# From the sixth unit on, attention products in 64x32 tiles with a query per partition, and x turned by VectorE blocks and DMAs through DRAM

## The chip, the core and the metric

The kernel runs on one core of a Trainium2 chip. The metric is the device time of one execution in microseconds; lower is better. Three executions of the kernel before took 380.43, 379.7 and 379.51 us, so its median is 379.7 us.

## What is computed

Two layers run one after the other. The first is attention in chunks: 4 batches, 8 heads, 768 positions, head size 64. A chunk of 32 queries sees 64 keys: 16 positions to its left, its own 32, 8 to its right, and 8 memory keys. The second mixes channels: it takes the attention output as x with 512 channels, blends each position with the one before it, and multiplies by three weight matrices.

```python
# attention, per chunk of 32 queries
scores = scale * q_c @ k_full.T            # 32 x 64 per head
a = softmax(scores)
out[:, :, c] = a @ v_full                  # 32 x 64 per head
# channel mix, x is (batch, 768, 512)
xk = mu_k * x + (1 - mu_k) * x_prev
xr = mu_r * x + (1 - mu_r) * x_prev
k = maximum(xk @ w_k, 0)
v = k * k @ w_v
r = sigmoid(xr @ w_r)
return r * v
```

Everything is in float32. Attention products run as float32 matmuls. The channel mix runs from unit 1 on as three float32r matmuls each (high part by high, high by low, low by high), and from unit 2 on the product with `w_v` is cut into seven smaller products.

## The kernel before, in words

The 3072 positions are cut into 12 units of 256 (`UTOK`), each of two tiles of 128 positions; a batch has three units. For each unit the following is done.

- **Scores.** `scores(u)` multiplies queries by keys: 64 matmuls in 64x32 tiles of the array (`s`, L463). One matmul has 64 contraction rows, 32 queries as the weights that are loaded, and 64 keys as the columns that are streamed. The result takes two PSUM banks (tag `s`, one buffer). VectorE then takes the maximum (L476), subtracts it (L481), ScalarE takes the exponential (L487), VectorE sums (L491 to L493) and normalizes (L497). The result is `e`.
- **Turning e.** From unit 3 (`MOVED`) on, `move(u)` turns e so that keys lie on partitions: VectorE turns 32x32 blocks (`eT`, L706), one DMA writes them to DRAM (`eD`, L713), and four DMAs read them back into `aTz` (L717). `aTz` holds the attention weights in two halves, one for each half of the partitions, with zeros in the other half.
- **Attention products.** In `attention(t)`, `f_a` multiplies values by attention weights: 16 matmuls per tile in 128x64 tiles of the array (`px`, L640), two tiles per unit. The values are the loaded weights, so the result has a channel per partition and a query per column: it is x already turned as the channel mix needs it. ScalarE copies it from PSUM into `xT` (L286, `f_x`), with one more column for the position before the unit (L654).
- **Blending.** `prep(u)` takes the difference of neighbours (`df`, L771) and blends (`xf`, L782, four instructions for each of two blends), then makes the high and low parts `xh` and `xl` (L286/L288, L803).
- **Channel mix.** `channel_mix(u)` holds four blocks `h0` to `h3` (`ph`, L1250, the product with `w_k`), two blocks `g0` and `g1` (`pr`, L1139, the gate), and `products(u)` the seven products `p1` to `p7` with `w_v` (`accx`, `accy`, `accz`, L1041), followed by additions (L1080, L1083) and multiplications by the gate (L1106, L1111, L1113) on VectorE and the stores.

TensorE's order is written out by hand. `LEAD` gives it up to unit 1; after that `STAGES` gives one line per unit u, a stage: `s` are the scores of unit u + 2, `a` and `b` the attention products of the two tiles of unit u + 1, `h0` to `h3` and `p1` to `p7` belong to unit u, and `g0` and `g1` to unit u + 1. A planner (`Plan`) orders the other engines around this: it gives each operation an estimated duration and a due time, and places them one by one. Its order is fixed when the program is built; on the chip each engine runs its own queue in order and waits on semaphores. All DMAs are issued from SyncE's queue.

Of the kernel before, what the change touches and what calls it, by code (L numbers as in the profile page):

```python
# [16 lines left out]
P = 128  # L17
# [19 lines left out]
LEAD = "s0.0.0 s0.0.1 s0.1 t0 t1 a0 s1.0 a1 h0.0.0 h0.0.1 h0.1.0 h0.2.0 h0.3.0 s1.1 h0.3.1 g0.0.0 g0.1.0 g0.0.1 h0.3.2 h0.3.3 g0.1.1 t2 t3 v0.0.0 a2 a3 v0.1.0 s2.0 v0.1.1 v0.0.1 h1.0.0 h1.0.1 h1.0.2 h1.0.3 h1.1.0 h1.1.1 t4 t5 h1.1.2 h1.1.3 a4 a5 v1.0.0 s3.0 g1.0 g1.1 v1.0.1 g2.0 g2.1 v1.1.0 v1.1.1"  # L37
STAGES = {
# [7 lines left out]
MOVED = 3  # L46
ROWS = [(0, 0, 1), (0, 1, 1), (1, 0, 2), (2, 0, 2), (3, 0, 2)]
# [158 lines left out]

def te_order():
# [3 lines left out]
    for u in range(1, nu):  # L211
# [5 lines left out]
        own.update(a=("a", 2 * u + 2), b=("a", 2 * u + 3), t=("t", 2 * u + 2), w=("t", 2 * u + 3), s=("s", u + 2, 0))  # L217
# [17 lines left out]
def local_attention__then__channel_mix(  # L235
# [372 lines left out]
    def attention(t, o_n, e):  # L608
# [56 lines left out]
        da = due["a", t]  # L665
# [20 lines left out]
    moved = {}  # L686

# [10 lines left out]
    def move(u, o_n, e):  # L698
# [16 lines left out]
        def f_in(x):  # L715
            s, z = x // 2, slice(CHUNK * x, CHUNK * (x + 1))
            nc.sync.dma_start(  # L717
                aTz[z, s].rearrange("p i n -> p (i n)").rearrange("p (j n) -> p j n", j=NJ),
# [5 lines left out]
        o_free = prior["a"]  # L724
# [4 lines left out]
    mix = {}  # L729

# [33 lines left out]
    def prep(u):  # L764
        deps = [xdone[u * QPU + c] for c in range(QPU)]
        ds = Slot("x4")

        def f_df(e):
            x = T["xT", u]
            d = T["df", u] = sb("x4", [P, KT, UTOK], f"df{u}")  # L770
            e.tensor_sub(d, x[:, :, 1:], x[:, :, :UTOK])  # L771

        if u not in OWN:
            o_d = op(either(u > 2, dve=(1.15, True), pool=(2.0, True)), f_df, deps, new=[ds], use=[xslot[u]])
        for m in (1, 0) if u > 1 else (0, 1):
            last = m == (u <= 1)

            def f_mix(m=m, last=last):
                d = T["df", u]
                f = T["xf", u, m] = d if last else sb("x4", [P, KT, UTOK], f"xf{u}")  # L780
                for k in range(KT):
                    nc.vector.scalar_tensor_tensor(  # L782
# [36 lines left out]
            else:  # L819
                o_d = op(("dve", 1.59, True), f_mix, [o_d, o_mu], new=[] if last else [fs], use=[ds, xslot[u]])  # L820
# [640 lines left out]
```

## Time and profile before

| | |
|---|---|
| median of three runs | 379.7 us |
| the profiled execution, its own time | 379.66 us |
| its span | 377.7 us |
| granted TensorE clock | 0.999 |
| busy: TensorE / VectorE / ScalarE / GpSimd | 98% / 82% / 59% / 1% of the span |
| TensorE matmul busy | 371.2 us |

The span runs from the first to the last instruction that the profiler shows; the execution's own time is about 2.0 us more. Shares of busy time are means over the whole span. From stage 5 on, at 180.88 us, the kernel repeats a stage of 29.1 us per unit until the scores run out in stage 10.

### The profile page before, as it was taken

How to read it: one execution, taken by the hardware profiler on the slowest of the kernel's cores; microseconds unless marked ns; L12 is line 12 of the kernel's file. 1: busy time of each engine (PE TensorE's matmuls, PEld its weight loads, DVE VectorE, ACT ScalarE, POOL GpSimd, SP SyncE). 2: the span in 40 equal slices, each digit the busy share in tenths (PEclk: the TensorE clock that was granted, in tenths of full speed). 3: DMA queues.
4: the chain of work that ended last, by engine and by line, in shares of the span. 5: the costliest groups of instructions: out<-in, count | busy, mean ns of one | idle time of the engine just before them, and what ended most of it. 6: DMA issues, size and time to landing. Idle time of an engine off the chain costs nothing.

```text
span 377.7 us, 10682 instructions
## 1 busy us (share of the span) xinstructions
PE 371.2 (98%) x4702; PEld 343.9 (91%) x4702; DVE 310.2 (82%) x499; ACT 221.7 (59%) x330; POOL 3.2 (1%) x11
## 2 busy tenths in 40 slices
PE   8999999999998999999999999999999999999996
PEld 6785579889998999999999999999999999999996
DVE  4899999999899599499599689689779879588264
ACT  2788998772682574475376276276276277256350
POOL 2000000000000000000000000000000000000000
PEclk9999999999999999999999999999999999999999
DMA  8999972513533723632731731751651332200101
GB/s 312 417 407 409 367 256 102 165 61 129 182 111 108 256 88 112 225 113 76 260 114 62 265 123 59 220 170 57 210 182 58 113 115 98 70 3 0 57 2 56
DMA packets 19822, 58.43 MB, mean 155 GB/s; under 512 B 2240, under 2 KB 7232, under 8 KB 19392
## 3 DMA queue, kind: packets, MB, share of 16 engines
q1 hardware_dynamic: 19776, 57.75, 42.7%
q8 instruction: 37, 0.61, 0.7%
q14 instruction: 9, 0.07, 0.1%
HBM read 46.73 MB, written 11.01 MB: 153 GB/s over the span
## 4 chain that ended last, share of the span: by engine, by line
PE 90%; DVE 4%; DMA 3%; SPq 1%; ACT 1%; issue 0%; DVEq 0%
PE ph L1250 29%; PE pr L1139 14%; PE accy L1041 10%; PE accx L1041 6%; PE accz L1041 6%; PE px L640 6%; PE pv L1352 4%; PE s L463 4%; PE ph L1196 4%; DMA vw<-in_vw_dram 3%; PE ph L1225 3%; PE pv L1339 2%; PE pr L1130 2%; DVE al L986 1%; PE pt L620 0%
## 5 line engine op out<-in xcount | busy, mean ns | idle before, releaser
L1250 PE MATMUL ph<-xh,wk 128*128 128x256 f32 x320 | 89.8, 281 | 0.0
L1250 PE MATMUL ph<-xl,wk 128*128 128x256 f32 x320 | 88.0, 275 | 0.0
L1250 PE MATMUL ph<-xh,wl 128*128 128x256 f32 x320 | 88.0, 275 | 0.0
L1269 ACT ACTIVATE kf<-ph 128x512 f32<-128x512 f32 x41 | 24.5, 597 | 90.0 <-PE ph L1250 88.3
L1250 PEld LDWEIGHTS ph<-xh,wk 128*128 128x128 f32 x320 | 61.3, 192 | 1.4
L1250 PEld LDWEIGHTS ph<-xh,wl 128*128 128x128 f32 x320 | 61.4, 192 | 0.0
L1250 PEld LDWEIGHTS ph<-xl,wk 128*128 128x128 f32 x320 | 61.4, 192 | 0.0
L286 ACT CAST ah<-kf 128x512 fp32r<-128x512 f32 x43 | 25.9, 620 | 23.3 <-DVE kf L964 22.0
L986 DVE TENSOR_TENSOR al<-kf,ah 128x512 fp32r<-128x512 f32 x50 | 33.8, 682 | 0.0
L1139 PE MATMUL pr<-wr,xh 128*128 128x512 f32 x88 | 33.5, 381 | 0.0
L1139 PE MATMUL pr<-wr,xl 128*128 128x512 f32 x88 | 33.4, 380 | 0.0
L1139 PE MATMUL pr<-wl,xh 128*128 128x512 f32 x88 | 33.4, 379 | 0.0
L1276 ACT ACTIVATE kf<-kf 128x512 f32<-128x512 f32 x48 | 30.0, 628 | 1.1
L640 PEld LDWEIGHTS px<-aTz,vw 128*64 128x64 f32 x768 | 23.5, 138 | 2.7 <-ACT w L348 0.8
L640 PE MATMUL px<-aTz,vw 128*64 128x64 f32 x768 | 25.2, 224 | 0.4 <-DMA vw<-in_vw_dram 0.4
L1041 PE MATMUL accx<-wv,ah 128*128 128x256 f32 x80 | 22.0, 275 | 0.0
L1041 PE MATMUL accx<-wl,ah 128*128 128x256 f32 x80 | 22.0, 275 | 0.0
L1041 PE MATMUL accx<-wv,al 128*128 128x256 f32 x80 | 22.0, 275 | 0.0
L1271 DVE TENSOR_SCALAR kf<-ph 128x512 f32<-128x512 f32 x7 | 4.8, 692 | 20.4 <-PE ph L1250 20.4
L1148 ACT ACTIVATE sg<-pr 128x512 f32<-128x512 f32 x24 | 14.2, 596 | 10.5 <-PE pr L1139 10.3
L1139 PEld LDWEIGHTS pr<-wr,xl 128*128 128x128 f32 x88 | 16.6, 189 | 2.5 <-DVE xl L803 0.2
L1139 PEld LDWEIGHTS pr<-wr,xh 128*128 128x128 f32 x88 | 16.7, 190 | 1.9
(149 smaller groups left out, 965.5 us busy)
## 6 DMA issues: line engine op xcount, KB each, us to landing
qk<-in_qk_dram SPq DMA_DIRECT2D x23, 768.0 KB, 6.7
vw<-in_vw_dram SPq DMA_DIRECT2D x24, 512.0 KB, 4.6
out_dram<-o SPq DMA_DIRECT2D x23, 256.0 KB, 2.4
eD<-eT SPq DMA_DIRECT2D x9, 512.0 KB, 2.6
aTz<-eD SPq DMA_DIRECT2D x36, 128.0 KB, 2.9
raw<-in_w_v_dram SPq DMA_DIRECT2D x4, 1024.0 KB, 9.4
raw<-in_w_k_dram SPq DMA_DIRECT2D x3, 1024.0 KB, 13.2
raw<-in_w_r_dram SPq DMA_DIRECT2D x2, 1024.0 KB, 8.7
```

The lines of the kernel that those rows point to most:

```text
L286: e.copy(dst, src)
L463: nc.tensor.matmul(s5[CHUNK * j : CHUNK * (j + 1), h, d - c, r, :], *operands(ts[d], r, j, slice(64 * h, 64 * h + 64)), start=True, stop=True,
L640: nc.tensor.matmul(p3[64 * h : 64 * h + 64, 2 * g : 2 * g + 2, CHUNK * j : CHUNK * j + CHUNK], v[:, g, h, j, :], a[:, h, g, j, :], start=True,
L986: nc.vector.tensor_sub(low(n), place[n](), T["ah", u, n].bitcast(F32))
L1041: nc.tensor.matmul(o, x, w, start=(n in fresh and c + i == 0), stop=(c == cs[-1] and i == 2), skip_group_check=True)
L1139: nc.tensor.matmul(pairs(p), x[:, k, c * P : (c + 1) * P], woven(w), start=(k + n == 0), stop=(k == KT - 1 and n == 2),)
L1148: nc.scalar.activation(sg, p, AF.Sigmoid)
L1196: nc.tensor.matmul(p[:, i * UTOK + c * P : i * UTOK + (c + n) * P], T["w", id(wk_hl[0]), k][:, fc], T["xf", u, 0][:, k, z], start=(i + k + ...
L1250: nc.tensor.matmul(pairs(p[:, i * UTOK : (i + 1) * UTOK]), w[:, fc], x[:, :, k].rearrange("p t n -> p n t"), start=(k + n == 0), stop=(k = ...
L1269: e.activation(part(), p, AF.Relu)
L1276: e.activation(q, q, AF.Square)
L1352: nc.tensor.matmul(pairs(p), x[:, tc_], woven(w), start=(f + n == 0), stop=(f == FT - 1 and n == 2),)
```

## The change

Units 0 to 4 stay as they are. From unit 5 (`ROWX`) on:

- The attention products swap their operands. The attention weights are now the loaded weights (64 keys by 32 queries) and the values are streamed (64 columns), in 64x32 tiles, 64 matmuls per unit. The result `px` has a query per partition, and takes the two PSUM banks of tag `s`, which the scores use too (one buffer for both).
- x then has to be turned. `rows_to_columns(u)` does it as `move` does for e: VectorE turns 32x32 blocks from PSUM into the free half of `aTz`, one DMA writes them to DRAM (`xD`), four DMAs read them back into `xT`. ScalarE's copies of `px` go.
- Chunks are placed in another order in the inputs (`chunk_order`), so that a unit's x comes out in order. `xT` then has the layout (chunk group, channel block, 64 positions) without the extra column, so `df` is made by three instructions (within 64 positions, between groups, and the first position, which reads the unit before).
- In `STAGES`, `z` are the scores of unit u + 3 and `x` the products of unit u + 2: both come one stage earlier than before. Stage 2 has `s` and `z`, stage 3 has `a`, `b` and `x`.
- `e` arrives in the first half of `aTz` alone and has one buffer (`aT5`).
- `LEAD` and the order of the products within a stage are new: p2 moves ahead of p6.

```diff
-    0: "s h0 h1 a b h2 h3 p1 p7 g0 p6 g1 p5 p2 p4 p3",
-    2: "h0 h1 s h2 a b h3 p1 p7 g0 p6 g1 p5 p2 p4 p3",
-    10: "h0 a b h1 h2 h3 p1 p7 g0 p6 p4 p5 p2 p3",
-    11: "h0 h1 h2 h3 p1 p7 g1 p6 p4a p5 p4b p3 p2",
+    0: "z h0 h1 x h2 h3 p1 p7 g0 p2 p6 g1 p5 p4 p3",
+    2: "h0 h1 s h2 a b p1 h3 p7 g0 p6 g1 p2 z p4 p5 p3",
+    3: "h0 a b h1 h3 z h2 p1 p7 g0 x g1 p6 p5 p2 p4 p3",
+    4: "z h0 h1 x h2 h3 p1 p7 g0 p2 p6 g1 p5 p4 p3",
+    9: "h0 h1 x h2 h3 p1 z g0 p7 p6 g1 p5 p2 p4 p3",
+    10: "h1 h0 h2 h3 p1 g0 p7 p6 p4 p5 p2 p3",
+    11: "h1 h0 h2 h3 p1 p7 g1 p6 p4a p5 p4b p3 p2",
...
+ROWX = 5
...
+            if u >= ROWX:
+                vload[t] = lv, vs
+                if c:
+                    rows_to_columns(u, landed, az, due["a", 2 * u])
+                return
...
+    def rows_to_columns(u, landed, az, da):
...
+            p = T["px", u] = ps("s", f"px{u}", QPU)
+            p = p.rearrange("p (r g c h d) -> p r g c h d", r=2, g=2, c=QPU, h=2)
...
+            for c in range(QPU):
+                v = T["vw", ts[c]].rearrange("p (g h j d) -> p g h j d", g=2, h=2, j=NJ)
+                for g in range(2):
+                    for h in range(2):
+                        for j in range(NJ):
+                            for i in range(2):
+                                z = slice(64 * i, 64 * i + 64)
+                                nc.tensor.matmul(
+                                    p[CHUNK * j : CHUNK * (j + 1), i, g, c, h, :], a[z, c, h, g, j, :], v[z, g, h, j, :],
+                                    start=True, stop=True,
+                                )
...
+        def f_turn():
+            t = turned_x
+            nc.vector.transpose(
+                t.rearrange("p (x m q) -> p x m q", x=X, m=M), T["px", u].rearrange("p (m x k) -> p x m k", m=M, x=X)
+            )
...
+        def f_out():
+            T["xD", u] = dram.tile([P, M * X * CHUNK], F32, tag="xD", name=f"xD{u}")
+            nc.sync.dma_start(T["xD", u], turned_x)
...
+            nc.sync.dma_start(
+                rows(u)[CHUNK * x : CHUNK * (x + 1)].rearrange("p j k n -> p j (k n)"),
+                T["xD", u].rearrange("(j p) (x n) -> x p j n", j=NJ, x=X)[x],
+            )
...
+                e.tensor_sub(d[:, :, :, 1:], back[:, :, :, : n - 1], back[:, :, :, 1:])
+                e.tensor_sub(d[:, :, 1:, 0], back[:, :, : NJ - 1, n - 1], back[:, :, 1:, 0])
...
+                    e.tensor_sub(d[:, :, 0, 0], rows(u - 1)[:, NJ - 1, :, n - 1], back[:, :, 0, 0])
```

**TensorE in the middle of stage 6** (between h1 and h2; the names are PSUM and SBUF tiles with their buffer numbers, and the last figure is how many equal instructions follow each other). Before, the two tiles of unit 7:

```order
L1250 MATMUL ph_1_2936<-xl_0_2816,wk_71 128x256
L1250 MATMUL ph_1_2936<-xh_0_2797,wl_740 128x256
L640 MATMUL px_2965<-aTz,vw_2582 64x2x32 x16
L640 MATMUL px_2984<-aTz,vw_2619 64x2x32 x16
L1250 MATMUL ph_2_3010<-xh_0_2797,wk_68 128x256
```

Now, unit 8:

```order
L1360 MATMUL ph_1_3170<-xl_0_3060,wk_71 128x256
L1360 MATMUL ph_1_3170<-xh_0_3028,wl_740 128x256
L726 MATMUL px_3202<-vw_2848,aTz 32x64 x32
L726 MATMUL px_3202<-vw_2852,aTz 32x64 x32
L1360 MATMUL ph_2_3271<-xh_0_3028,wk_68 128x256
```

At the same place 32 matmuls into two PSUM tiles became 64 matmuls into one.

**VectorE at the end of stage 5 and the start of stage 6.** Before, from the last addition after p5 (`o_1<-accy`) to the maximum of the next scores:

```order
L1083 TENSOR_TENSOR o_1_2722<-accy_2727,o_1_2722 128x256
L1111 TENSOR_TENSOR o_0_2695<-accx_2665,sg_2322 128x256
L803 TENSOR_TENSOR xl_0_2816<-df_2623,xh_0_2797 128x1024
L1083 TENSOR_TENSOR o_1_2722<-accz_2682,o_1_2722 128x256
L1106 TENSOR_TENSOR o_1_2722<-o_1_2722,sg_2322 128x512
L1083 TENSOR_TENSOR o_0_2695<-accy_2727,o_0_2695 128x256
L1113 TENSOR_TENSOR o_0_2695<-o_0_2695,sg_2322 128x256
L474 MEMSET s_0_2833 32x2x4x8
L476 TENSOR_REDUCE mx_0_2928<-s_0_2833 128x16
```

Now:

```order
L1193 TENSOR_TENSOR o_1_2970<-accy_2974,o_1_2970 128x256
L733 STREAM_TRANSPOSE aTz<-px_2746 128x1024
L913 TENSOR_TENSOR xl_0_3060<-df_2844,xh_0_3028 128x1024
L1193 TENSOR_TENSOR o_1_2970<-accz_2913,o_1_2970 128x256
L1193 TENSOR_TENSOR o_0_2928<-accy_2974,o_0_2928 128x256
L1216 TENSOR_TENSOR o_1_2970<-o_1_2970,sg_2512 128x512
L1221 TENSOR_TENSOR o_0_2928<-accx_2896,sg_2512 128x256
L1223 TENSOR_TENSOR o_0_2928<-o_0_2928,sg_2512 128x256
L486 MEMSET s_0_3064 32x2x4x16
L490 TENSOR_REDUCE mx_0_3161<-s_0_3064 128x16
```

The turning of x (L733) stands between the addition after p5 and `xl_0`, the low part that h0 of the next stage reads; the multiplication that reads `accx` moved back.

**TensorE where p6 ends, in stage 3.** `accy` is the PSUM bank that p6 fills and p5 goes on with; VectorE reads it in between. Before, p6 and then g1:

```order
L1041 MATMUL accy_1890<-mh_1212,ah_3_1864 128x256
L1041 MATMUL accy_1890<-ml_1214,ah_3_1864 128x256
L1041 MATMUL accy_1890<-mh_1212,al_3_1881 128x256
L1139 MATMUL pr_1_1907<-wr_76,xh_1_1822 128x512
L1139 MATMUL pr_1_1907<-wl_859,xh_1_1822 128x512
```

Now, p6 and then p5 (its operands are `t1h` and `tl`):

```order
L1151 MATMUL accy_2064<-mh_1212,ah_3_1960 128x256
L1151 MATMUL accy_2064<-ml_1214,ah_3_1960 128x256
L1151 MATMUL accy_2064<-mh_1212,al_3_1963 128x256
L1151 MATMUL accy_2064<-t1h,ah_3_1965 128x256
L1151 MATMUL accy_2064<-tl,ah_3_1965 128x256
```

In this stage alone nothing stands any more between p6 and p5; in all other stages g1 or p4 still does.

## Rows read from the trace of the kernel before

**Rows 1.** The page: busy time by engine, and the chain that ended last.

```profile
PE 371.2 (98%) x4702; PEld 343.9 (91%) x4702; DVE 310.2 (82%) x499; ACT 221.7 (59%) x330; POOL 3.2 (1%) x11
...
PE 90%; DVE 4%; DMA 3%; SPq 1%; ACT 1%; issue 0%; DVEq 0%
```

**Rows 2.** TensorE's waits: total us, times, longest (start of kernel aside).

```profile
PE accy L1041 <- DVE o L1083: 1.1, 1, 1.1
PE px L640 <- DMA vw<-in_vw_dram: 0.4, 1, 0.4
```

**Rows 3.** Busy time by engine in stage 5: us (instructions), clock, DMA share.

```profile
180.88:209.97 29.09, 29.09 (x397) 28.05 (x396) 24.05 (x40) 16.23 (x23) 0.00 (x0) 1.00 0.43 146
```

**Rows 4.** Timeline of TensorE in stage 5: start, duration, matmuls.

```profile
180.88 1.48 PE L463 MATMUL s<-qk 64*32 64x64 f32 x128
182.29 0.38 PE L1250 MATMUL ph<-xh,wk 128*128 128x256 f32 x1
...
187.84 2.09 PE L640 MATMUL px<-aTz,vw 128*64 128x64 f32 x64
189.86 0.38 PE L1250 MATMUL ph<-xh,wk 128*128 128x256 f32 x1
```

**Rows 5.** Groups by line on VectorE and ScalarE, for the added and removed work.

```profile
L476 DVE TENSOR_REDUCE mx<-s 128x16 f32<-128x1024 f32 (+1 forms) x12 | 14.1, 1175 | 1.4 <-PE s L463 1.1
...
L286 ACT COPY xT<-px 128x512 f32<-128x512 f32 x24 | 13.6, 584 | 1.6 <-PE px L640 1.4
...
L771 DVE TENSOR_TENSOR df<-xT 128x1024 f32<-128x1024 f32 x10 | 12.2, 1220 | 5.8 <-ACT xT L286 5.8
...
L706 DVE STREAM_TRANSPOSE eT<-e 128x1024 f32<-128x1024 f32 x9 | 11.2, 1239 | 0.0
...
L492 DVE TENSOR_SCALAR sum<-sum 128x16 f32<-128x16 f32 (+1 forms) x12 | 2.1, 174 | 0.4
```

**Rows 6.** Timeline of VectorE from stage 5 into stage 6.

```profile
187.95 0.69 DVE L1271 TENSOR_SCALAR kf<-ph 128x512 f32<-128x512 f32 x1 [3.07 <-PE ph L1250]
189.51 0.43 DVE L288 CAST ah<-kf 128x512 fp32r<-128x512 f32 x1 [0.87 <-ACT kf L1276]
...
191.06 1.22 DVE L771 TENSOR_TENSOR df<-xT 128x1024 f32<-128x1024 f32 x1
...
196.13 1.16 DVE L803 TENSOR_TENSOR xl<-xf,xh 128x1024 fp32r<-128x1024 f32 x1
...
206.70 0.42 DVE L1083 TENSOR_TENSOR o<-accy,o 128x256 f32<-128x256 f32 x1
207.40 0.42 DVE L1111 TENSOR_TENSOR o<-accx,sg 128x256 f32<-128x256 f32 x1 [0.28 <-PE accx L1041]
207.74 1.32 DVE L803 TENSOR_TENSOR xl<-df,xh 128x1024 fp32r<-128x1024 f32 x1
```

**Rows 7.** DMA issues: count, KB each, median us from issue to landing.

```profile
eD<-eT SPq DMA_DIRECT2D x9, 512.0 KB, 2.6
aTz<-eD SPq DMA_DIRECT2D x36, 128.0 KB, 2.9
```

**Rows 8.** Timeline of SyncE's queue: the four loads of the turned e.

```profile
206.34 1.79 SPq L717 DMA_DIRECT2D aTz<-eD  x4
```

**Rows 9.** Timeline of VectorE and TensorE at the end of stage 2.

```profile
120.13 0.41 DVE L1083 TENSOR_TENSOR o<-accy,o 128x256 f32<-128x256 f32 x1
...
120.69 0.35 PE L1041 MATMUL accy<-wv,ah 128*128 128x256 f32 x1 [1.11 <-DVE o L1083]
```

**Rows 10.** Timeline of the lead, around the second attention product.

```profile
13.70 1.17 ACT L286 COPY aTz<-pt 64x512 f32<-64x512 f32 x2
...
14.19 0.86 PE L463 MATMUL s<-qk 64*32 64x64 f32 x64
...
15.48 1.15 PE L640 MATMUL px<-aTz,vw 128*64 128x64 f32 x32 [0.43 <-DMA vw<-in_vw_dram]
```

More of the change, by code (lines that the diff above doesn't have):

```diff
@@ L204, in turn, with chunk_order @@
         return done
+def chunk_order(b):
+    seen = []
+    for u in range(S // UTOK):
+        n = b * (S // UTOK) + u
+        seen += [QPU * NJ * u + (QPU * j + c if n >= ROWX else NJ * c + j) for c in range(QPU) for j in range(NJ)]
+    return seen
 def te_order():
@@ L688, in after, with rows @@
+    def rows(u):
+        return T["xT", u].rearrange("p k n -> p (k n)")[:, : KT * UTOK].rearrange("p (j k n) -> p j k n", j=NJ, k=KT)
     def after(t, o_a, s3, f_x, da):
@@ L729, in local_attention__then__channel_mix, with place_of @@
     mix = {}
+    def place_of(u):
+        return [k // 2 + k % 2 * 2 if u >= ROWX else k for k in range(KT)]
     def f_rest():
@@ L764, in prep @@
     def prep(u):
-        deps = [xdone[u * QPU + c] for c in range(QPU)]
+        deps = xland.get(u) or [xdone[u * QPU + c] for c in range(QPU)]
         ds = Slot("x4")
+        at = place_of(u)
         def f_df(e):
@@ L770, in f_df @@
             d = T["df", u] = sb("x4", [P, KT, UTOK], f"df{u}")
+            if u >= ROWX:
+                x, d, n = rows(u), d.rearrange("p k (j n) -> p k j n", j=NJ), UTOK // NJ
+                back = x.rearrange("p j k n -> p k j n")
+                e.tensor_sub(d[:, :, :, 1:], back[:, :, :, : n - 1], back[:, :, :, 1:])
+                e.tensor_sub(d[:, :, 1:, 0], back[:, :, : NJ - 1, n - 1], back[:, :, 1:, 0])
+                if units[u][1] == 0:
+                    e.tensor_scalar_mul(d[:, :, 0, 0], back[:, :, 0, 0], -1.0)
+                elif u == ROWX:
+                    past = T["xT", u - 1][:, :, UTOK].rearrange("p (g r) -> p r g", r=2)
+                    e.tensor_sub(
+                        d[:, :, 0, 0].rearrange("p (r g) -> p r g", r=2), past, back[:, :, 0, 0].rearrange("p (r g) -> p r g", r=2)
+                    )
+                else:
+                    e.tensor_sub(d[:, :, 0, 0], rows(u - 1)[:, NJ - 1, :, n - 1], back[:, :, 0, 0])
+                return
             e.tensor_sub(d, x[:, :, 1:], x[:, :, :UTOK])
         if u not in OWN:
-            o_d = op(either(u > 2, dve=(1.15, True), pool=(2.0, True)), f_df, deps, new=[ds], use=[xslot[u]])
+            wait = u >= ROWX and units[u][1] > 0
+            if wait:
+                deps = deps + (xland.get(u - 1) or [xdone[u * QPU - 1]])
+            o_d = op(
+                either(dve=(1.15 + 0.35 * (u >= ROWX), True)), f_df, deps, new=[ds], use=[xslot[u]] + [xslot[u - 1]] * wait
+            )
         for m in (1, 0) if u > 1 else (0, 1):
@@ L781, in f_mix @@
                 for k in range(KT):
+                    if u >= ROWX:
+                        z, x = slice(at[k], at[k] + 1), rows(u)[:, :, k]
+                        d3, f3 = (a[:, k].rearrange("p (j n) -> p j n", j=NJ) for a in (d, f))
+                        nc.vector.scalar_tensor_tensor(f3, d3, mu_sb[:, 2 + m, z], x, ALU.mult, ALU.add)
+                        continue
                     nc.vector.scalar_tensor_tensor(
@@ L819, in prep @@
             else:
-                o_d = op(("dve", 1.59, True), f_mix, [o_d, o_mu], new=[] if last else [fs], use=[ds, xslot[u]])
+                o_d = op(("dve", 1.59, True), f_mix, [o_d, o_rest], new=[] if last else [fs], use=[ds, xslot[u]])
             wide = int(m == 0 and u > 1)
@@ L1420, with placed @@
     nch = S // CHUNK
+    places = [chunk_order(b) for b in range(B)]
+    def placed(a):
+        return np.stack([a[b][:, places[b]] for b in range(B)])
     def windows(a, mem):
```

42 lines of the change are left out of this document (33 added, 9 removed), and 2 rows, old and new, of the table bufs.

## The prediction

> **What bounds the kernel now.** I read the page first: TensorE is busy 98% of the span and holds 90% of the chain that ended last [rows 1]. Then TensorE's own waits: after the first microsecond only two are above 0.35 us, 1.1 us on VectorE and 0.4 us on a DMA [rows 2]. So whatever TensorE no longer has to do comes off the time, and whatever it must newly wait for goes on. [...]
>
> **What the change takes from TensorE.** Before, the attention products of a unit start at 187.84 and the next matmul at 189.86: 2.02 us [rows 4]. The new products are 64 matmuls, each with 64 contraction rows, 32 loaded columns and 64 streamed columns, in 64x32 tiles, writing 32 partitions by 64 columns into two banks, with the eight tiles of the array taken in turn. The scores have exactly this form: `64*32`, 64x64. They take from 180.88 to 182.29, 1.41 us, between the same kinds of neighbours [rows 4]. I take 1.41 us for the new products. The bounds are 1.35 (no row shows this form faster; 0.06 for reading) and 2.02 (nothing gained). Units 5 to 11 have the new form, seven units: 7 x (2.02 - 1.41) = **4.27 us less**. Units 0 to 4 keep theirs.
>
> [...] The products of a unit were 64 matmul records in 2.02 us, 31.6 ns each; the scores are 128 records in 1.41 us, 11 ns each [rows 4]. [...]
>
> **What it gives VectorE and ScalarE.** Added per unit: one turning of 128x1024 from PSUM. The same turning from SBUF takes 1239 ns, and a maximum over as many elements from PSUM 1175 [rows 5]; I take 1.24 us, with 1.2 and twice that, 2.5, as bounds. The difference becomes three instructions: 16x63 elements at the old 1.22 us, and two of 4 to 12 elements at the 0.17 us of the nearest small one [rows 5], 0.35 us more; bounds 0.2 and 1.0, should the strided rows run slower. Blends keep their count and sizes. Removed: two copies of 0.58 us on ScalarE [rows 5], which costs and gives nothing, since ScalarE idles 13 us a stage. So VectorE goes from 24.05 to about 25.6 us of a stage of 28.5 us. That is hidden if it comes at the right place, which depends on order.
>
> **Does VectorE deliver in time?** Let E be the end of a stage, where the next scores start. The new turning must free the PSUM tile that those scores write: this is the new wait. It stands right behind the addition after p5 (`o_1<-accy`). Behind p5 come p4 and p3; two products took 2.67 us in stage 5 (before, p4 and p3 ran from about 207.3, where the multiplication waited for p2, to 209.97) [rows 3, 6], so p5 ends at E - 2.67. VectorE's own queue gets there at: the first activation of a stage waits for h1, and the addition came 18.75 us behind it, 206.70 - 187.95, with hardly a gap [rows 6]. In the new order the same work stands between, less a cast of 0.43 us and plus 0.35 us of difference. The activation starts 7.07 us into the stage, so the addition can start at 25.82; p5 ends at 28.48 - 2.67 = 25.81. Both arrive together. Then: addition from E - 2.56, turning from E - 2.2 to E - 1.0. **The scores have 0.9 to 1.0 us to spare.** Then `xl_0`, 1.32 us [rows 6], ends at E + 0.3; h0 starts at E + 1.41: 1.1 us to spare. The gate g0 is reached 0.6 us earlier than now, `xl_1` is ready as now: it ends at 197.29, while h2 and h3 (as long as h0 and h1, 5.55 us) and two products put g0 at 189.86 + 5.55 + 2.67 = 198.1 [rows 4, 6]. Of these 0.8 us 0.2 remain, and g0 first runs two matmuls that don't read `xl_1`. The rest of VectorE's tail (additions and multiplications, 2.2 us) ends at E + 2.4, 0.9 us later than the maximum could start; behind it 3.07 us of idle time before the activation absorb that [rows 6].
>
> **The DMAs.** xD waits for the turning and issues at E - 0.9; it lands 2.6 us later if it is like eD [rows 7]. The four loads of x stand in SyncE's queue behind the two stores, the last of which waits for VectorE's tail: issue from E + 2.5, 1.8 us for the four [rows 8], landing 2.9 us after the last issue [rows 7], at E + 7.2. The difference that reads x starts 10.18 us into the stage now (191.06) [rows 6], some 9.8 after the change. So 2.6 us are spare, and behind these loads only the next scores' and values' loads wait, which have most of a stage.
>
> **The places that are not the stage.** In stage 3 p5 follows p6 at once. VectorE must add p6's bank first: 0.11 us until it starts (187.84 to 187.95), 0.41 us, and 0.15 us until TensorE goes on (120.54 to 120.69) [rows 4, 6, 9]: +0.65 us, certain. In stage 2 p3 waited 1.11 us for VectorE's addition [rows 2, 9]; now the scores of unit 5 (1.41 us) stand ahead, but VectorE also runs a different order there. I take 0.9 us, -0.2, with -1.1 and +0.5 as bounds. Some product in stage 2 may now wait for its low part: +0.2. In the lead the second attention product moves ahead of the scores that stood before it; it waited for its values until 15.48. These now load one place earlier, but ScalarE's copies end only at 14.87 [rows 10], so TensorE idles from about 14.2 to 14.95 instead of 0.43 us: +0.35. Warm-up matmuls are as many as before. Sum: +1.0 us.
>
> **Sum.** 379.66 (the profiled execution, 0.04 below the median) - 4.27 + 1.0 = **376.4 us**. Its own range, with VectorE's bounds and those of the waits, is 375.2 to 378.0.
>
> **Rivals.**
> 1. *VectorE late (the slower side).* Place: the scores at each stage's start, behind the turning of x, and five of them follow a new product directly (stages 4 to 8). If the turning takes 2.5 us instead of 1.24, it ends at E + 0.25 and each scores starts 0.35 late: 5 x 0.35 = 1.8, 378.2 us. The kernel gets slower by over 0.3% when each is over 0.9 us late, a turning of 3.1 us. For it: VectorE's order has no gap ahead of it. Against: all its rows of this size lie within 1.17 to 1.24 us. At a lateness of 1.4 us: 383.4 us.
> 2. *A price per matmul.* If a record keeps its 31.6 ns, the products take 4.04 us, 7 x 2.02 more: 394.8 us with the other terms. The scores' rows speak against it. [...]
> 3. *x lands late.* Above 2.6 us of lateness, each microsecond holds the difference, `xl_1` and g0 in up to six stages. With 3 us more, 0.4 x 6 = 2.4 us come back: 378.8 us, about no change. The same loads of aTz at 2.9 us speak against it.
> 4. *Stalls vanish:* if stage 2's wait goes and the lead loses nothing, 375.0 us.
>
> **Chances.** The forecast 0.78, the stalls that vanish 0.09 (both faster by over 0.3%, 1.1 us, which is about what a measurement tells from no change), x late or VectorE a little late 0.08 (within 0.3%), VectorE late throughout 0.04, a price per matmul 0.01. So faster 0.87, same 0.08, slower 0.05. The range takes in the vanishing stalls and VectorE's longer turning: 374.8 to 378.6.
>
> **What would show it.** Right: TensorE's row for px in 64x32 at 1.4 us a unit; the turning of px at 1.2 to 1.3 us; stages of 28.5 us; one wait of 0.5 to 0.7 us of `accy` in stage 3. Wrong: TensorE waiting in each stage for the turning (scores) or for `xl_1` (g0), px rows above 1.6 us a unit, or a difference that waits for the DMA of xT.

## The result, and the profile after

The new kernel takes 383.86 us (median of eight runs, 381.32 to 386.80) against 379.96 us (379.47 to 380.65): ratio 1.010, 95% interval 1.006 to 1.015. It is slower by 1.0%; 376.4 us were forecast. Its runs also spread over 5.5 us, those of the kernel before over 1.2 us. The profiled execution took 382.04 us, a span of 380.2.

The page first: busy time by engine, two of the DMA queues (packets, MB, share of 16 engines), and the chain that ended last (for before, [rows 1]).

```profile
PE 369.3 (97%) x5150; PEld 339.6 (89%) x5150; DVE 318.5 (84%) x518; ACT 213.2 (56%) x311; POOL 2.4 (1%) x9
...
q1 hardware_dynamic: 24816, 65.09, 47.6%
q8 instruction: 40, 0.66, 0.8%
...
PE 90%; DVE 6%; issue 2%; ACT 1%; DVEq 0%
```

TensorE's busy time fell by 1.9 us and VectorE's rose by 8.3, as forecast in direction. New is "issue 2%" in the chain: TensorE waited for nothing that the profile shows. Its waits say where (total us, times, longest); they answer to [rows 2]:

```profile
PE px L726 <- issue: 2.7, 1, 2.7
PE ph L1360 <- issue: 1.3, 3, 0.8
...
PE accy L1151 <- DVE o L1193: 1.2, 2, 0.6
PE px L654 <- ACT aTz L300: 0.7, 1, 0.7
PE s L477 <- issue: 0.5, 1, 0.5
```

The kernel before has no TensorE matmul that waits for "issue". No line names VectorE's turning or the DMA of x. Stage by stage (4 to 7, from the start of the scores to that of the next; columns as in [rows 3]):

```profile
155.97:185.25 29.28, 28.75 (x461) 27.52 (x460) 25.11 (x41) 15.99 (x22) 0.00 (x0) 1.00 0.54 190
185.25:216.70 31.45, 28.74 (x461) 27.51 (x460) 25.12 (x43) 15.72 (x22) 0.00 (x0) 1.00 0.50 169
216.70:245.71 29.01, 28.76 (x461) 27.50 (x461) 24.95 (x43) 15.87 (x22) 0.00 (x0) 1.00 0.54 183
245.71:275.22 29.51, 28.76 (x461) 27.50 (x460) 24.68 (x42) 15.97 (x22) 0.00 (x0) 1.00 0.53 180
```

29.09 us less 0.61 for the products is 28.48. These four stages are 0.8, 3.0, 0.5 and 1.0 us longer, 5.3 us in all. Each holds one wait for "issue" (0.53, 2.71, 0.25 and 0.75 us), and each is some 0.27 us longer still than its wait explains: TensorE is busy 28.75 us in them, against 28.50 in stages without such a wait (e4_final, below). A fifth wait stands in stage 8:

```profile
284.90 0.38 PE L1360 MATMUL ph<-xl,wk 128*128 128x256 f32 x1 [0.25 <-issue]
```

It costs 0.5 us in the same way: from the last scores to TensorE's end the new kernel takes 101.93 us, and e1_noxdma, without this wait, 101.40. With 7 x 0.61 = 4.27 us off, 0.83 us lost by the start of stage 2 (97.86 against 97.03 us), the wait of 0.52 us in stage 3 and 0.46 us less wait in stage 2, the sum is 2.5 us more; the two profiled executions differ by 2.4.

The largest wait, on TensorE's timeline in stage 5 (as [rows 4]):

```profile
192.02 0.28 PE L1360 MATMUL ph<-xh,wl 128*128 128x256 f32 x1
192.22 1.42 PE L726 MATMUL px<-vw,aTz 64*32 64x64 f32 x120
196.34 0.32 PE L726 MATMUL px<-vw,aTz 64*32 64x64 f32 x8 [2.71 <-issue]
196.59 0.38 PE L1360 MATMUL ph<-xh,wk 128*128 128x256 f32 x1
```

TensorE stops after 120 of the 128 records of one product, in the middle of a run of matmuls of which none waits for an operand. What is special about that place shows when instructions are counted from wait to wait (busy time and count of matmuls, then of weight loads, and so on):

```profile
157.93:196.34 38.41, 35.70 (x634) 34.26 (x634) 30.99 (x52) 21.31 (x29) 0.00 (x0) 1.00 0.61 211
196.34:230.06 33.72, 33.47 (x508) 32.12 (x507) 27.45 (x49) 17.49 (x25) 0.00 (x0) 1.00 0.51 176
230.06:249.15 19.09, 18.33 (x254) 17.29 (x254) 18.19 (x31) 8.77 (x13) 0.00 (x0) 1.00 0.38 137
249.15:284.90 35.75, 35.50 (x634) 34.03 (x635) 27.70 (x46) 21.00 (x29) 0.00 (x0) 1.00 0.52 173
```

Matmuls and loads together: 1268, 1015, 508 and 1269, that is about 5, 4, 2 and 5 times 254. The views leave out TensorE's semaphore instructions. Counted in the trace with these, the distances are 1280, 1025, 512 and 1280, which is 5, 4, 2 and 5 times 256, to one instruction. So the waits of this kernel stand at a grid of 256 instructions; 256 of them are called a block below. The q8 queue has 40 packets of 0.66 MB / 40 = 16.5 KB for 10,300 matmul and load records, one for each 257; before, it had 37 for 9404, one for each 254:

```profile
q8 instruction: 37, 0.61, 0.7%
```

By this count the packets are read here as TensorE's program. Two windows of the DMA view around the largest wait, the first up to 193.90, the second from there to 194.95:

```profile
q1 hardware_dynamic: 303, 0.79, 94.6%
q14 instruction: 1, 0.01, 1.1%
```

```profile
q1 hardware_dynamic: 67, 0.35, 98.9%
q8 instruction: 1, 0.02, 6.1%
```

From 191.25, where a block begins, no q8 packet moves, while data keep the DMA engines 95% busy (0.79 MB in 2.65 us). TensorE stops at 193.64; the packet moves from 193.90 on, and TensorE goes on at 196.34, 1.4 us behind its end. In all five waits it goes on 1.3 to 1.5 us behind the end of a packet, 2.3 to 3.3 us behind its start.

### The profile page after: what moved, and what is told of

It is laid out like the page before. It is cut to its first block, busy times and chain, and to the rows that moved or that the text cites. A ratio compares the mean times of both kernels' runs of the same rounds, so it can differ in the third digit from the quotient of the medians.

```text
span 380.2 us, 11617 instructions
## 1 busy us (share of the span) xinstructions
PE 369.3 (97%) x5150; PEld 339.6 (89%) x5150; DVE 318.5 (84%) x518; ACT 213.2 (56%) x311; POOL 2.4 (1%) x9
## 4 chain that ended last, share of the span: by engine, by line
PE 90%; DVE 6%; issue 2%; ACT 1%; DVEq 0%
PE ph L1360 28%; PE pr L1249 14%; PE accy L1151 10%; PE accx L1151 6%; PE accz L1151 6%; PE pv L1462 4%; PE s L477 4%; PE ph L1306 4%; PE ph L1335 3%; PE px L726 3%; PE px L654 3%; PE pr L1240 2%; PE pv L1449 2%; PE warm L1517 1%; PE pt L634 1%
## 5 line engine op out<-in xcount | busy, mean ns | idle before, releaser
L300 ACT CAST ah<-kf 128x512 fp32r<-128x512 f32 x48 | 29.6, 621 | 28.1 <-DVE kf L1074 14.7
L1386 ACT ACTIVATE kf<-kf 128x512 f32<-128x512 f32 x44 | 27.4, 629 | 1.0
L477 PEld LDWEIGHTS s<-qk 64*32 64x32 f32 x1472 | 15.4, 105 | 3.6 <-issue 2.6
L1249 PEld LDWEIGHTS pr<-wl,xh 128*128 128x128 f32 x88 | 16.7, 190 | 1.8
L477 PE MATMUL s<-qk 64*32 64x64 f32 x1472 | 17.6, 225 | 0.6 <-issue 0.5
```

The lines of the kernel that those rows point to most:

```text
L300: e.copy(dst, src)
L477: nc.tensor.matmul(s5[CHUNK * j : CHUNK * (j + 1), h, d - c, r, :], *operands(ts[d], r, j, slice(64 * h, 64 * h + 64)), start=True, stop=True,
L1249: nc.tensor.matmul(pairs(p), x[:, place_of(u)[k], c * P : (c + 1) * P], woven(w), start=(k + n == 0), stop=(k == KT - 1 and n == 2),)
L1386: e.activation(q, q, AF.Square)
```

## The experiments

The theory: TensorE runs dry (has no instruction left to run) where a block of 256 instructions is used up faster than the next one comes. Scores and new products are such places, since 64 matmuls of this form are 128 matmul and 128 load records, a whole block in 1.41 us (the old products were half a block in 2.02). It also holds that busy DMA engines delay the next block, and the change adds 1 MB of x traffic per stage. Two other explanations stand against it. Rival 1: the dense burst alone does it. Rival 2: data, VectorE or the lead (the part ahead of stage 2). Medians, and ratios to the kernel before on the same chip:

| kernel | us | ratio (95%) |
|---|---|---|
| e1_noxdma | 379.20 | 0.997 (0.995 to 0.999) |
| e1_shift | 393.30 | 1.032 (1.028 to 1.036) |
| e1_split | 383.87 | 1.009 (1.006 to 1.011) |
| e1_late | 379.78 | 0.999 (0.997 to 1.001) |
| e2_traffic | 379.84 | 0.999 (0.998 to 1.000) |
| e2_twice | 406.11 | 1.065 (1.062 to 1.069) |
| e2_late4 | 381.21 | 1.003 (1.001 to 1.005) |
| e2_late4s | 382.27 | 1.006 (1.004 to 1.008) |
| e3_best | 380.77 | 1.000 (0.998 to 1.001) |
| e3_bestl | 379.72 | 0.998 (0.997 to 1.000) |
| e3_lead | 381.41 | 1.003 (1.001 to 1.006) |
| e4_nocut | 378.90 | 0.997 (0.995 to 0.999) |
| e4_final | 377.39 | 0.993 (0.991 to 0.994) |

**e1_noxdma: the x traffic taken away.**

```diff
-            nc.sync.dma_start(T["xD", u], turned_x)
+            nc.sync.dma_start(T["xD", u][:, :4], turned_x[:, :4])
...
+                T["xT", u][CHUNK * x : CHUNK * (x + 1)], T["xD", u][CHUNK * x : CHUNK * (x + 1), :4]
...
+        return T["xT", u].unsqueeze(2).unsqueeze(3).to_broadcast([P, NJ, KT, 64])
```

> The new kernel without its x traffic: the turned x is still written and read back by one and four DMAs, at the same places of the same queue, but four numbers per partition each (2 KB instead of 512 KB each way), and the blend reads these four numbers, spread over the unit, instead of x, so what is left out is the moving of x. Instructions and their order are those of the new kernel on every engine. Theory (TensorE runs out of instructions: the loads of its next 256 instructions share the DMA engines with the data, and the added 1 MB per stage delays them): the waits put down to issue, 4.5 us in the new kernel's profile, fall below 2 us, none above 1 us, and the time falls to 377 to 378.5 us, ratio 0.993 to 0.997 to the kernel before. Rival 1 (a dense burst of instructions is too much by itself, whatever the DMA engines carry): the waits stay at 157.9, 196.3, 249.2 and 284.9 us, time 381 to 384, ratio 1.003 to 1.010. Rival 2 (VectorE or the lead holds TensorE, the waits are a by-product): unchanged, ratio 1.006 to 1.014.

The waits put down to issue fell from 4.5 to 1.5 us, and all that remains is one, in the scores:

```profile
PE s L478 <- issue: 1.5, 1, 1.5
```

The kernel leaves out the moving of x. The waits in and behind the products are gone from the view with the same instructions in the same order (stages 5 to 7 take 28.49, 28.79 and 28.66 us), so rival 1 alone doesn't explain them, and rival 2's VectorE (busy 318.0 us against 318.5) and lead, both unchanged, don't either. The time is 0.7 us above the upper end of what was expected: the scores' wait grew from 0.5 to 1.5 us.

**e1_shift: the grid moved by half a block.**

```diff
+                        for y in range(32):
+                            nc.tensor.matmul(warm[:32, :64], zero_sb[:64, :32], zero_sb[:64, :64], start=True, stop=True)
```

> The new kernel with 32 more tiny matmuls (64 contraction rows, 32 loaded and 64 streamed columns of zeros) ahead of the first warm-up matmul, nothing else. They are 128 instructions of TensorE (64 matmul records, 64 load records), half of 256, and cost at most 0.7 us at the start, where TensorE waits for its first data. In the new kernel all waits put down to issue above 0.2 us stand whole multiples of 256 TensorE instructions apart. Theory and rival 1 (instructions come in blocks of 256, and a block that is used up in 2 to 3 us leaves TensorE dry): every wait moves by half a block: none any more at 158, 196, 249 and 285 us; new ones at the end of the products of unit 6 (about 166 us), at the scores of unit 11 (about 275 us), behind the products of unit 11 (about 311 us), perhaps behind those of unit 5 (about 145 us), 1 to 3 us each where the DMA engines are busy. Time 380 to 386. Rival 2 (data, VectorE or the lead): the waits stay where they are and the time moves by 0 to 0.7 us.

The tiny matmuls cost not 0.7 but 7.0 us at the start (64 records in one tile, 110 ns each), so the time says nothing. The places do. The starts of the stages are 6 to 9 us later here, and no wait is left at the old five places. The new ones, besides one of 0.7 us in the lead, are in the gate behind the products of unit 5 (155.76, 0.9 us), behind those of unit 6 (175.50, 0.7) and in the scores of unit 11 (284.19, 0.6), as expected, and at 264.73 (1.7), which was not. The expected one behind unit 11's products did not come. In the trace both go with the q8 packet: that of the block which ends at 264.73 moved only 3.4 us after the block's start, with the DMA engines 96% busy until then, and that of the block of unit 11's products, used up in 2.25 us, moved 1.3 us ahead of the block's start. The windows between them, columns as before:

```profile
155.76:175.50 19.74, 18.53 (x381) 17.51 (x382) 15.04 (x25) 7.94 (x10) 0.00 (x0) 1.00 0.68 220
175.50:264.73 89.23, 87.54 (x1395) 84.10 (x1396) 77.21 (x133) 47.51 (x66) 0.00 (x0) 1.00 0.54 191
264.73:284.19 19.46, 18.85 (x254) 17.93 (x253) 17.52 (x29) 10.40 (x15) 0.00 (x0) 1.00 0.29 101
```

763, 2791 and 507 are 3, 11 and 2 times 254. The waits follow the instruction count and not the work: rival 2 is out as what sets their places.

**e1_split: half of the products one block later.**

```diff
+                held.append(lambda: f_a([1]))
...
-            for c in range(QPU):
+            for c in cs:
...
+            rest = held.pop() if held and o.eng == "pe" else None
...
+            if rest:
+                rest()
```

> The new kernel with the products of x cut in two: the 32 matmuls of the unit's first tile stay where they are, the 32 of its second tile come one block later on TensorE (behind h2, or behind g1 in stage 3). Nothing else moves, no engine has more or less to do, and the DMAs carry the same. A block of 256 instructions then never holds more than half a burst of products. Theory and rival 1: the waits in or behind the products (196.3, 230.1, 284.9 us) go, those in or behind the scores (157.9: 0.5 to 0.7 us, 249.2: 0.8 to 0.9 us) stay; 3.7 us come back, time 378 to 379, ratio 0.994 to 0.998. Rival 2 (the added traffic, VectorE or the lead): 381 to 384, ratio 1.003 to 1.012.

In the profiled execution (381.36 us) the waits in and behind the products are gone, and 1.1 us in the scores is the only one named. But the time is 4.9 us above the upper end of what was expected. Part of it I had left out: a half takes 0.78 us from its start to that of the next matmul, not 0.70 (TensorE's timeline, the second half of one unit).

```profile
197.73 0.86 PE L729 MATMUL px<-vw,aTz 64*32 64x64 f32 x64
198.51 0.38 PE L1363 MATMUL ph<-xh,wk 128*128 128x256 f32 x1
```

That is 1.1 us in seven units. Four of the other runs lie at 383.4 to 384.8 us without a profile, two of them at a granted clock of 0.996 and two at 1.0; what they waited for is open.

**e1_late: the products where the DMA engines are idle.**

```diff
+                held.append([3, lambda: f_a(True)])
...
+            was = list(held) if o.eng == "pe" else []
...
+                x[0] -= 1
+                if x[0] == 0:
+                    held.remove(x)
+                    x[1]()
```

> The new kernel with the products of x three places later on TensorE from unit 6 on (behind p1 instead of behind h1, some 7 us), where the DMA engines carry little (8 GB/s and less between 201 and 211 us in the new kernel's profile, 340 GB/s at 193 to 199 us); nothing else moves. The blocks of 256 are then used up fastest in the products of unit 6 (2.7 us), unit 8 (3.2 us) and unit 11 (1.5 us). Theory (dense burst and busy DMA engines together): a load of instructions that meets no data is through in about 2.5 to 3 us, so each of the three waits is below 1 us; the waits in the scores (158 and 249 us) stay; time 377.5 to 379, ratio 0.993 to 0.998. Rival 1 (density alone): waits in the products as large as now, up to 2.7 us, time 381 to 384. Rival 2: unchanged, 381 to 384.

As the theory had it, apart from 0.8 us: with the same bursts and the same bytes, the waits in the products fall to one of 0.3 us, and the kernel is 1.1% faster than the new one by the two ratios. The three blocks of its products that are used up fastest, in 2.8, 3.2 and 2.2 us at DMA engines 39%, 3% and 0% busy, have that one wait between them (0.33 of the 2.2 us). The scores' wait was 2.2 us this time, and its windows (before it, behind it, later) show a second cost of such a wait, the granted clock:

```profile
156.69:160.33 3.64, 1.43 (x123) 1.26 (x123) 2.33 (x5) 0.00 (x0) 0.00 (x0) 1.00 0.59 219
160.33:163.80 3.47, 3.47 (x20) 3.29 (x20) 2.45 (x2) 0.00 (x0) 0.00 (x0) 0.51 0.47 155
163.80:167.00 3.20, 3.20 (x31) 3.20 (x30) 0.00 (x0) 1.81 (x3) 0.00 (x0) 1.00 0.84 245
```

**e2_traffic: the x traffic put into the kernel before.**

```diff
+                    for z in range(2):
+                        nc.sync.dma_start(T["xD", u][:, 512 * z : 512 * z + 512], T["o", u, 1])
...
+                    for x in range(4):
+                        nc.sync.dma_start(
+                            xS[32 * x : 32 * x + 32].rearrange("p (j n) -> p j n", j=4),
+                            T["xD", u].rearrange("(j p) (x n) -> x p j n", j=4, x=4)[x],
```

> The kernel before with x traffic added that nobody uses: at the end of each of stages 4 to 10 a DMA more of 512 KB to DRAM (the finished output tile, twice) and behind the stores four loads of 128 KB that read it back in pieces of 1 KB into a free buffer, as the new kernel does with x. Every engine's instructions, TensorE's above all, are those of the kernel before. Theory (a wait needs both: a block of 256 instructions used up in 2 to 3 us, and busy DMA engines): in the kernel before, only two blocks are used up in under 3 us, at 122 and 151 us, ahead of the added traffic; so TensorE gets no wait put down to issue above 0.5 us, and the time is 379.5 to 381, ratio 0.998 to 1.003. Rival (the traffic alone slows the kernel, by late loads of qk and vw and a longer SyncE queue): 382 to 385, ratio 1.006 to 1.014.

The traffic alone cost nothing here (ratio 0.999), where blocks last longer: behind the start of the added traffic none is used up in under 3 us. The run's two waits put down to issue, 0.4 and 0.3 us, stand ahead of it, where the kernel before uses up blocks fastest.

**e2_twice: only a denser program, no x traffic.**

```diff
-                for d in ds:
+                for d in list(ds) * (1 + (u >= 7)):
```

> The kernel before with the scores of units 7 to 11 computed twice in a row, into the same place: 512 TensorE instructions in a row in 2.8 us instead of 256 in 1.41 us, five times, without any x traffic and with the old products. By TensorE's time alone 5 x 1.41 = 7.1 us more: 387 us, ratio 1.019. Theory and rival 1 (instructions come in blocks of 256): each of the five doubled bursts holds a whole block, which is used up in 1.41 us while the next one needs 2.4 to 3.4 us to come; so each has one wait of 1 to 2 us put down to issue in the scores, and the time is 392 to 397 us, ratio 1.032 to 1.045. If TensorE's instructions were never short without the x traffic: 387 us and no such waits.

Five whole blocks in a burst, five waits, each in the scores:

```profile
PE s L463 <- issue: 12.3, 5, 2.9
```

And the granted clock fell behind each of them, to 0.54 behind the first (the last 1.55 us of its wait of 2.20, then the 3.65 us behind it) and to 0.50 to 0.68 for some 3.5 us behind the others:

```profile
183.90:185.45 1.55, 0.00 (x0) 0.00 (x0) 0.00 (x0) 0.00 (x0) 0.00 (x0) 1.00 0.80 227
185.45:189.10 3.65, 3.65 (x36) 3.53 (x36) 2.45 (x2) 0.00 (x0) 0.00 (x0) 0.54 0.83 296
```

The places were right and the price too low: 2.5 us for each wait, not 1 to 2, and a mean granted clock of 0.975 over the execution, which I had not counted. So these waits, in blocks that are wholly one burst, came without the x traffic. This kernel's own data still move beside it: from the block's start to the wait's end the DMA engines were 73% to 81% busy in the first three and 35% and 37% in the last two, whose waits (2.9 and 2.5 us) are no shorter.

**e2_late4 and e2_late4s: products four places later; then the grid moved too.** The first is the edit of e1_late with 4 for 3; the second adds, for two of the warm-up matmuls:

```diff
+                        for y in range(42):
+                            w = CHUNK * (y % 4)
+                            nc.tensor.matmul(
+                                warm[w : w + CHUNK, :64], zero_sb[:64, :CHUNK], zero_sb[:64, :64], start=True, stop=True
+                            )
```

> The new kernel with the products of x four places later on TensorE from unit 6 on (behind p7 instead of behind h1, some 8.4 us later, where the DMA engines are idle); nothing else moves. Blocks of 256 that are used up in under 2 us: one in the scores of unit 6, one in those of unit 7 (158 us in the new kernel) and one in the products of unit 6; one of 2.5 us in the scores of unit 10. Theory: little different from three places later: waits in the scores at 158 and 249 us, below 1 us in the products of unit 6; 378.5 to 380.5, ratio 0.995 to 1.001. Rival 1 (density alone): 1.5 us and more in the products of unit 6 too; 380 to 382.

> The kernel with the products of x four places later, and 42 tiny matmuls (64 contraction rows, 32 loaded and 64 streamed columns of zeros, four tiles of the array in turn) in the place of the first two warm-up matmuls: TensorE's blocks of 256 instructions are cut 160 instructions earlier, and nothing else is changed. By count, the fastest block from stage 2 on is then used up in 2.5 us (the scores of unit 9), the next in 2.8 us, all others in 3 us and more, where without the tiny matmuls four are under 2.5 us. Theory: the waits put down to issue fall to below 1 us in all; time 377 to 378.5, ratio 0.992 to 0.996, and runs agree as closely as those of the kernel before. Rival (the cutting into blocks plays no role): as without them, and the tiny matmuls add 0 to 1 us at the start: 378.5 to 381.

Both missed. Four places later is worse than three (1.003 against 0.999): 1.1 and 0.8 us of issue, and new waits for ScalarE (1.1), a load of qk (0.9) and VectorE (0.5). With the grid moved, the issue waits behind the lead fell to one of 0.9 us, as counted; but two new ones, 1.3 and 2.0 us, came into the lead, where the DMA engines carry 320 to 430 GB/s, with the granted clock at 0.50 behind the second (from 20.90 to 24.20). The shift at the start moved the grid in the lead too.

**e3_best, e3_bestl, e3_lead: the grid moved behind the lead; the lead before.** 84 matmuls of 512 columns, three gates and unit 1's products with w_v, are each made two of 256 (the diff shows the gates), which adds 168 instructions and by the rows costs some 0.5 us (0.216 us for one of 512 columns against 2 x 0.111). In e3_best and e3_bestl unit 5's products also move behind p6:

```diff
+CUT = ((2, 0), (2, 1), (3, 0))
...
+                    for t in (slice(0, P), slice(P, 2 * P)) if (u, c) in CUT else (slice(0, DM // 2),):
+                        nc.tensor.matmul(
+                            pairs(p)[:, t], x[:, place_of(u)[k], c * P : (c + 1) * P],
+                            woven(w)[:, t] if (u, c) in CUT else woven(w),
...
+                held.append([3 if u > ROWX else 2, lambda: f_a(True)])
```

> The new kernel with three edits. The products of x of units 6 to 11 come three places later (as in the run with the late products, 379.8 us). Those of unit 5 come between p6 and p5 of stage 3, where TensorE waited 0.5 us for VectorE's addition. And 168 TensorE instructions are added at next to no time behind the lead: 84 matmuls with 512 columns (the products with w_v of unit 1, three gates of units 2 and 3) are each cut into two with 256 columns, 0.216 us against 2 x 0.111 by the rows, 0.5 us in all. By count, the blocks of 256 instructions used up in under 3 us behind the lead are then two (2.1 us in the scores of unit 9, 1.9 us in the products of unit 10, where the DMA engines are quiet) instead of seven. Theory: the waits put down to issue sum up to less than 2 us, none at 158 us, no fall of the granted clock; time 377 to 378.5, ratio 0.990 to 0.995. Rival (where the blocks are cut plays no role): 379.3 to 380, ratio 0.997 to 0.999.

> The same three edits, and LEAD as in the kernel before. By the two traces the new LEAD had cost 0.8 us by the start of stage 2 (97.86 against 97.03 us). If that comes from the order in the lead: 0.5 to 0.8 us less than with the new LEAD, 376.3 to 378. If it is chance of the run: the same time within 0.3 us.

> The new kernel with LEAD alone as in the kernel before; stages, products and x traffic are the new ones. TensorE's instructions are one more, so the blocks are cut as in the new kernel. Theory (the loss is in the blocks, the lead costs 0.5 to 0.8 us of it): 381 to 386 with the same spread, ratio 1.003 to 1.012. Rival 2 in the form that the new LEAD holds the whole loss: 376 to 378, ratio 0.990 to 0.995.

The waits put down to issue fell to 0.5 and 0.3 us, but the time didn't follow. In e3_bestl TensorE waited for VectorE instead (the first two lines), which waited for x (the third, a row of its timeline):

```profile
PE accz L1155 <- DVE al L1100: 1.6, 1, 1.6
...
PE pr L1254 <- DVE xl L917: 0.9, 1, 0.9
```

```profile
169.31 1.21 DVE L863 TENSOR_TENSOR df<-xT 128x1008 f32<-128x1008 f32 x1 [3.54 <-DMA xT<-xD]
```

SyncE's queue shows why. In the new kernel the loads of vw and of x stood at

```profile
145.18 0.95 SPq L628 DMA_DIRECT2D vw<-in_vw_dram  x2
...
159.94 2.28 SPq L744 DMA_DIRECT2D xT<-xD  x4
```

Moving unit 5's products behind p6 held the loads of vw, which write where these products read, and e and x stood behind them:

```profile
149.47 0.95 SPq L629 DMA_DIRECT2D vw<-in_vw_dram  x2
150.52 0.38 SPq L794 DMA_DIRECT2D eD<-eT  x1
157.02 2.58 SPq L798 DMA_DIRECT2D aTz<-eD  x4
159.70 0.38 SPq L743 DMA_DIRECT2D xD<-aTz  x1
160.17 1.24 SPq L1200 DMA_DIRECT2D out_dram<-o  x2
164.87 1.75 SPq L748 DMA_DIRECT2D xT<-xD  x4
```

This is the prediction's rival 3 (x lands late), made by my own edit. The old LEAD gave 1.05 us between the medians of e3_best and e3_bestl, a little more than expected. e3_lead, the new kernel with the old LEAD, keeps the waits put down to issue (7.0 us in its profile, which is of its slowest run, 385.51 us, at a granted clock of 0.996) and stays slower than the kernel before (1.001 to 1.006): the lead isn't the whole loss. Its ratio is 0.7% below the new kernel's, 2.7 us, where the traces give the lead 0.4 to 1.6 us; no run separates the rest from the waits, which vary by more than that from run to run.

**e4_final and e4_nocut: the same kernel on two grids.** Old LEAD, products three places later from unit 6 on, unit 5 left alone; e4_final has the cut matmuls, e4_nocut hasn't.

> The new kernel with LEAD as in the kernel before, the products of x of units 6 to 11 three places later, and 84 matmuls of 512 columns behind the lead cut into two of 256 each (168 TensorE instructions more, some 0.5 us); the products of unit 5 stay where the new kernel has them, since moving them behind p6 held SyncE's queue (the loads of vw wait for them, and the turned e and x behind these) and made TensorE wait 1.5 and 1.05 us for VectorE in stage 4. By count two blocks of 256 are used up in under 3 us (2.0 us each). Theory: those 2.5 us go, the wait of 0.7 us in stage 3 is back: 377 to 378.5 us, ratio 0.991 to 0.995, and runs agree within some 1.5 us. Rival (how the blocks are cut plays no role): the same as its twin without the cut matmuls, less 0.5 us for these.

> The same kernel without the cut matmuls: every engine has the same work in the same order, and the DMAs too; only TensorE's blocks of 256 instructions are cut elsewhere. By count six blocks are used up in under 3 us behind the lead (1.6, 2.0, 2.6, 2.4, 1.6 us, and one of 3.2). Theory: waits put down to issue in the scores near 158 us (1 to 2.5 us) and 249 us, and some 0.5 us in the products of unit 11; in a part of the runs the granted clock falls behind the first one; 378.5 to 380.5, 1 to 2.5 us more than its twin. Rival: 0.5 us less than its twin.

Both as expected, apart from a wait in the products of unit 11 that e4_nocut's profile doesn't show. The twins differ by 1.5 us (ratios 0.991 to 0.994 and 0.995 to 0.999, on one chip), and the one with more matmuls is the faster: what changed between them is where the blocks are cut. e4_nocut's runs reach from 377.48 to 381.38 us, e4_final's from 376.84 to 377.80. e4_nocut's waits put down to issue are the first two lines; e4_final has one:

```profile
PE s L477 <- issue: 1.1, 1, 1.1
PE ph L1363 <- issue: 0.9, 1, 0.9
```

```profile
PE ph L1366 <- issue: 0.7, 1, 0.7
```

And e4_final's stages 4 to 7, where the new kernel had 29.28, 31.45, 29.01 and 29.51 us:

```profile
155.69:184.19 28.50, 28.50 (x462) 27.43 (x461) 24.93 (x41) 15.76 (x22) 0.00 (x0) 1.00 0.58 187
184.19:212.68 28.49, 28.49 (x461) 27.42 (x461) 24.86 (x43) 15.73 (x22) 0.00 (x0) 1.00 0.55 187
212.68:242.10 29.42, 28.76 (x461) 27.50 (x460) 24.93 (x43) 15.75 (x22) 0.00 (x0) 1.00 0.54 180
242.10:270.60 28.50, 28.50 (x462) 27.43 (x461) 24.65 (x42) 15.78 (x22) 0.00 (x0) 1.00 0.55 182
```

Three of four are the forecast 28.48 us to within 0.02. With 65 MB of data over the DMA engines as in the new kernel, it beats the kernel before by 0.7% and the new one by some 1.7% (0.993 / 1.010).

**All profiles together.** The kernels here have 36 waits of over 0.15 us put down to issue. Counted with the semaphore instructions from the first that a trace holds, all 36 have 193 or 194 instructions and a whole number of times 256 ahead of them, whatever the work there is, and all 36 end 1.2 to 1.6 us behind the end of a q8 packet. That a fast block alone isn't enough shows in the new kernel too: the scores that start at 134.73 us use up a block in 1.72 us without a wait. There the DMA engines were 7% busy, and the packet had moved 1.7 us ahead of the block's start.

## Why the prediction was wrong

**What held.** The products take 1.41 us (192.22 to 193.64 for 120 records, 193.67 to 195.08 for all 128 in e1_noxdma) against 2.02 [rows 4]. The turning takes 1.24 us and ends at E - 1.0 in stage 5:

```profile
183.02 1.24 DVE L733 STREAM_TRANSPOSE aTz<-px 128x1024 f32<-128x1024 f32 x1
```

Scores and gates never waited for VectorE, the joint of p6 and p5 cost 0.52 us (0.65 forecast), stage 2's wait fell from 1.11 to 0.65 us. In the stages that repeat, x landed in time; VectorE's difference waited for it once (3.2 us at 335.5, near the end), and TensorE not behind it. The prediction's rival 1 (VectorE late) did not happen; its rival 3 only where e3_best brought it about. The lead was mis-sized: 0.35 forecast, 0.83 by the two traces; four other profiles with the new lead reach stage 2 at 98.3 to 98.6 us, four with the old one at 97.0 to 97.5. The 0.2 us for a product of stage 2 that waits for its low part did not come. Partly by luck these errors cancel: the terms for stages 2 and 3 and the lead sum up to 0.9 us (0.52 - 0.46 + 0.83), where 1.0 was forecast. So what the sum lacked is the five waits for "issue", 5.9 us with what they cost behind them: 376.3 us without them against 382.04 in the profiled execution. The median lies another 1.8 us above that execution, and no profile of such a slower run of the new kernel was taken.

**The step that failed** is the first conclusion: "So whatever TensorE no longer has to do comes off the time, and whatever it must newly wait for goes on", with only the waits that semaphores name. By the theory that these runs bear out, TensorE also waits for its own program, a term that the sum put at nothing. The prediction counted the records of the new products (128 in 1.41 us) and weighed a price per record, its rival 2; what the runs show is a price per block of 256, paid at some blocks only, by the theory those that were used up before the next one came: five in the new kernel's profile, 4.5 us of waits. The scores from which 1.41 us was read are just as dense, but there were half as many bursts per stage, and by luck of the grid only two blocks of the kernel before were used up in under 3 us (2.2 and 2.8 us), neither with a wait in [rows 2].

**The second half of the same omission** is in the paragraph on the DMAs. It costed 1 MB of x per stage at nothing, since behind these loads "only the next scores' and values' loads wait". But at the largest wait a q8 packet moved only after 2.65 us of data at 95% of the DMA engines, 0.26 us behind TensorE's stop. e1_noxdma prices that: with the bytes taken away the waits put down to issue fall from 4.5 to 1.5 us. e2_traffic shows that the bytes without the dense products cost nothing (ratio 0.999), e2_twice that dense bursts wait without the added bytes (12.3 us in five waits), beside the data that the kernel before moves anyway, and e1_late that the products are nearly free where the DMA engines are idle (one wait of 0.33 us in three blocks, at 0% to 39%). In the new kernel both causes act together.

Not settled: what sets the scores' wait near 158 us, 0.5 to 2.6 us in seven kernels with the same cuts there. In the traces it goes with the q8 packet, which moves 0.2 to 2.5 us after the block's start; this does not follow the DMA engines' load alone, since without the x traffic (e1_noxdma) it was 1.4 us. Also open is what the slower runs of e1_split and of the new kernel waited for.

## What to carry to other kernels

Count an engine's instructions as a load of their own: where the trace shows instruction packets, divide the records by the packets, and look for places where a whole packet's worth is used up within a few microseconds (2.4 us ahead of the largest wait here), above all next to heavy DMA traffic (95% there). Where TensorE waits for "issue" at a constant distance in instructions, move the dense work to where the DMA engines are quiet, or move the grid by cutting matmuls that cost little to cut (84 of them, 0.5 us by the rows here); e4_final gained 1.7% over the new kernel with these two and the old lead, and nothing taken out of the work. And read the spread of the runs: it grew here from 1.2 to 5.5 us, before any trace was opened.

## What the runs showed of the hardware

- A whole block in one burst cost TensorE 2.2 to 2.9 us a time in e2_twice (12.3 us in five waits), without any added DMA traffic, at DMA engines 35% to 81% busy. In the new kernel a block used up in 1.72 us had no wait, at DMA engines 7% busy.
- Behind some of the waits of 2.0 to 2.9 us the granted clock fell to about half (0.51 for 3.47 us in e1_late behind 2.2 us, 0.50 for 3.30 us in e2_late4s behind 2.0, 0.54 for 3.65 us in e2_twice behind 2.2). At 0.51 3.47 us lose some 1.7 us, so that by this estimate e1_late's wait of 2.2 us cost nearly twice its length. The wait of 2.71 us in the new kernel's profile had no such fall (1.00 in its whole stage). Of the new kernel's eight runs, the four at a granted clock of 0.995 or 0.996 took 383.6 to 386.8 us, the four at 0.999 or 1.0 took 381.3 to 384.1.
- 64x32 matmuls took 11 ns a record where the eight tiles of the array take turns (128 records in 1.41 us). All in one tile, writing to one place, they took 110 ns each, at a granted clock of 1.00:

```profile
1.18 7.03 PE L1519 MATMUL warm<-zero_sb 64*32 64x64 f32 x64 [1.18 <-DVE zero_sb L290]
```

In four tiles in turn, also at 1.00, 84 records took 2.5 us, 30 ns each (e2_late4s). Whether the tile or the place in PSUM sets the difference was not tried.
